# Attention with linear distance biases and a gated channel mix: softmax weights of tiles 9 to 23 transposed as rounded float32

## The chip, the core and the metric

The kernel is one program on one of the eight cores of a Trainium2 chip. The metric is device time in microseconds (us), from launch to end, as the median of several runs; lower is better. A profile of one further execution gives the times of single instructions. The engines are called PE (matrix products, with its weight loads shown apart as PEld), DVE (vectors), ACT (activation functions), POOL (general) and SP, which in this kernel issues almost all transfers. SPq, PEldq and so on are the instruction streams of these engines.

## What is computed

Four sequences of 768 positions pass through eight heads of causal attention of width 64, in which a query sees the last 96 keys and the first 8, with a bias that falls linearly with distance. The joined heads (512 wide) go through a channel mix.

```
scores = q @ k.T / 8 - slope[h] * dist       # outside the window: -1e9
a = exp(scores - max) / (sum + 1e-9)
x = (a @ v), heads joined                    # 4 x 768 x 512
xk = mu_k * x + (1 - mu_k) * x_prev          # xr likewise with mu_r
out = sigmoid(xr @ w_r) * (relu(xk @ w_k)**2 @ w_v)
```

## The kernel before

The 4 x 768 positions are 24 tiles of 128 queries (`NTILES`), six to a sequence. A tile needs two blocks of 128 keys: its own and the one before, in which the first 32 columns are replaced by the sequence's first keys. The first tile of a sequence (0, 6, 12, 18) needs one block only. Two tiles make a chunk, and the channel mix runs over 12 chunks of 256 positions.

A loop runs over steps; step n has four parts `hp` = 0 to 3, each for two heads. In a part PE does, in this order, the transposes of tile n-1 for the two heads (`transposes`, L331), the score products of tile n (`scores`, L298 to L302), and then a share of the channel mix of an earlier chunk (L391 to L393), taken from a generator piece by piece. At the start of a step PE multiplies the transposed weights of tile n-2 with the values (`weighted`, L348).

The path of one head's weights: PE writes the scores `s`; DVE adds the bias and takes the row's maximum (L309, into `e`); ACT takes the exponential and its sum (L310); DVE makes the reciprocal of the sums for four heads at a time (L316, L317); POOL multiplies the weights by it (L320). PE then transposes each 128 x 128 block of `e` into PSUM (`t`), ACT copies it out (`et`, L332), and PE multiplies. Up to tile 6 (`NATIVE` = 7) the scores are plain float32 products; from tile 7 on operands are split into a rounded part and a rest, both in the rounded float32 type (`F32R`), and a score takes two products (L301, L302). The channel mix takes three products of that type for each one.

In a transpose, `e` is the operand that is loaded into PE as weights, and the identity matrix `ident` streams past it; in the profile's rows the streamed operand is named first (`t<-ident,e`), and `s<-kw,qh` likewise has `qh` loaded and `kw` streamed.

Buffers of a pool go round. `e` has 10, one `kk` or `sig` of the channel mix takes one of 4 (`f2_pool`), and the split weights of the channel mix take 20 of the 21 of `w_pool` for the whole run once they are made, so that one is over.

SP issues its transfers strictly in the order of its list, and each waits there for what it needs: a load (`qraw`, `kraw`, `va`) for its buffer, an output (`out_dram<-sig`, L462) for the product before it. A scheduler places the instructions of every engine when the program is built; where it puts them is shown below in its own rows.

At the very end, seven small DVE instructions (L638 to L644) test the sizes of the window for a general path that these inputs don't need; each engine loads the result (L646) and branches over that path (L647).

Of the kernel before, what the change touches and what calls it, by code (L numbers as in the profile page):

```python
# [22 lines left out]
NTILES = B * NT  # L23
NCHUNK = NTILES // 2
NATIVE = 7
GMAX = 32
LMAX = 97
NEG = -1.0e9
# [4 lines left out]
def tile_biased_attention_channel_mix(ctx: ExitStack, tc: tile.TileContext, qT, kT, v, n_sizes, mu_kr, w_k, w_v, w_r, q_rows, k_rows, v_rows, slopes, out):  # L33
# [15 lines left out]
        vec.scalar_tensor_tensor(sizes, low, 0.0, high, op0=ALU.is_lt, op1=ALU.add)  # L49
        vec.scalar_tensor_tensor(sizes, sizes, 4294967296.0, low, op0=ALU.mult, op1=ALU.add)  # L50

    ident = const.tile([128, 128], F32, name="ident")
    make_identity(nc, ident)

    mus = const.tile([128, 2, 4], F32, name="mus")
    mus1 = const.tile([128, 2, 4], F32, name="mus1")
# [22 lines left out]
    ps_a = fast.enter_context(tc.tile_pool(name="ps_a", bufs=1, space=PSUM))  # L79
    ps_f = fast.enter_context(tc.tile_pool(name="ps_f", bufs=3, space=PSUM))  # L80


    zeros = const.tile([128, 256], BF16, name="zeros")
    vec.memset(zeros, 0.0)
# [89 lines left out]
    def weight_split(i):  # L174

        name, src, k, c = w_steps[i]
        word, hi = w_word.pop((name, k, c)), w_hi[name][:, k, c : c + 512]
        lo = w_low[name, k, c] = w_pool.tile([128, 512], F32R, tag="wl", name=f"w{name}_lo_{i}")
        (act.copy if i % 4 < 2 else pool_copy)(hi, word)
        if last[0] is None:  # L180
            vec.tensor_sub(lo, word, hi)  # L181
        else:
            with tc.issue_after(last[0]):
                vec.tensor_sub(lo, word, hi)

    w_count = [0, 0]
# [1 line left out]
    def weights_go(begun):  # L188
        while w_count[0] < min(begun, len(w_steps)):
            weight_begin(w_count[0])  # L190
            w_count[0] += 1
# [94 lines left out]
    def scores(n, hp):  # L286
# [31 lines left out]
        for u in range(nh):  # L318
            e = s["e"][h0 + u]
            pool.tensor_scalar(e[:, :w], e[:, :w], r[:, u : u + 1], 1.0, op0=ALU.mult, op1=ALU.mult)  # L320

    def transposes(n, hp):
        s = state[n]
        nb = 2 if n % NT else 1
        pt = ps_t.tile([128, 512], F32, name=f"t_{n}_{hp}", tag="t")
        et = et_pool.tile([128, 512], F32, name=f"et_{n}_{hp}", tag="et")
        for u in range(2):
            e = s["e"].pop(2 * hp + u)
            for k in range(nb):
                c = (u * nb + k) * 128  # L330
                pe.transpose(pt[:, c : c + 128], e[:, k * 128 : (k + 1) * 128], ident)  # L331
        act.copy(et[:, : 2 * nb * 128], pt[:, : 2 * nb * 128])  # L332
        s["et", hp] = et

# [45 lines left out]
            vec.scalar_tensor_tensor(x[:, j, :], xc[:, j, :], m[:, j : j + 1], x[:, j, :], op0=ALU.mult, op1=ALU.add)  # L380
        return x

    def channel_mix(xk, xr, out_rows, f_pool, f2_pool, ps_f, first=False):
        if first:
            kk_all = f_pool.tile([128, 8, 256], F32, name="kk_0", tag="kk_hi")
        else:
            kkh = f_pool.tile([128, 8, 256], F32R, name="kk_hi", tag="kk_hi")
            kkl = f_pool.tile([128, 8, 256], F32R, name="kk_lo", tag="kk_lo")

        def three(o, sh, sl, mh, ml, first, last):  # L390
            pe.matmul(o, sh, mh, start=first, stop=False)  # L391
            pe.matmul(o, sh, ml, start=False, stop=False)  # L392
            pe.matmul(o, sl, mh, start=False, stop=last)  # L393

        def z_of(i):
            z = ps_f.tile([128, 512], F32, name="z", tag="f")
            c = slice(i * 128, (i + 1) * 128)
            for k in range(4):
                if first:
                    pe.matmul(z, xr[:, k, c], w_word["r", k, 0], start=k == 0, stop=k == 3)  # L400
                else:
                    three(z, xr[0][:, k, c], xr[1][:, k, c], w_hi["r"][:, k, :], w_low["r", k, 0], k == 0, k == 3)
                yield
            sig = f2_pool.tile([128, 512], F32, name="sig", tag="f2")
            sigs.append((z, sig))

        sigs = []
        for fp in range(4):
            if first:
                weights_go(4 if fp < 2 else 8)  # L410
            else:
                splits_go(4 if fp < 2 else 8)
            ps = ps_f.tile([128, 512], F32, name="kp", tag="f")
            for u in range(2):
                f = slice((2 * fp + u) * 128, (2 * fp + u + 1) * 128)
                c = fp // 2 * 512
                g = slice(f.start - c, f.stop - c)
                o = ps[:, u * 256 : (u + 1) * 256]
                for k in range(4):
                    if first:  # L420
                        pe.matmul(o, w_word["k", k, c][:, g], xk[:, k, :], start=k == 0, stop=k == 3)
                    else:
                        three(o, w_hi["k"][:, k, f], w_low["k", k, c][:, g], xk[0][:, k, :], xk[1][:, k, :], k == 0, k == 3)
                    if k % 2:
                        yield
            kk = f2_pool.tile([128, 2, 256], F32, name="kk", tag="f2")
            pv = ps.rearrange("p (a q) -> p a q", a=2)
            act.activation(kk, pv, AF.Relu)  # L428
            if first:
                vec.tensor_mul(kk_all[:, 2 * fp : 2 * fp + 2, :], pv, kk)  # L430
                if fp % 2:
                    splits_ok[0] = 2 * fp + 2
            else:
                vec.tensor_mul(kk, pv, kk)  # L434
                act.copy(kkh[:, 2 * fp : 2 * fp + 2, :], kk)  # L435
                vec.tensor_sub(kkl[:, 2 * fp : 2 * fp + 2, :], kk, kkh[:, 2 * fp : 2 * fp + 2, :])  # L436
        if first:
            weights_go(12)
        else:
            splits_go(12)  # L440
        for i in range(2):
            yield from z_of(i)
        if first:
            splits_ok[0] = 12
        for z, sig in sigs:
            act.activation(sig, z, AF.Sigmoid)
        for i in range(2):
            c = slice(i * 128, (i + 1) * 128)
            vp = ps_f.tile([128, 512], F32, name="vps", tag="f")
            sig = sigs[i][1]  # L450
            for f in range(8):
                if first:
                    weights_go(13 + f)
                    pe.matmul(vp, kk_all[:, f, c], w_word["v", f, 0], start=f == 0, stop=f == 7)
                    if i:
                        splits_ok[0] = 13 + f
                else:
                    splits_go(13 + f)
                    three(vp, kkh[:, f, c], kkl[:, f, c], w_hi["v"][:, f, :], w_low["v", f, 0], f == 0, f == 7)
                yield  # L460
            last[0] = vec.tensor_mul(sig, vp, sig).ins
            nc.sync.dma_start(out_rows(i), sig)  # L462

    splits_ok = [0]
    last = [None]

    def ffn(c):
        xt = state["x", c]
        if c:
            xk, xr = (mix(xt[:, :, 1:257], xt[:, :, 0:256], tag, p4k, f_pool) for tag in "kr")  # L470
        else:
            xk, xr = (plain_mix(xt[:, :, 1:257], xt[:, :, 0:256], tag) for tag in "kr")
        return channel_mix(xk, xr, lambda i: out[(2 * c + i) * 128 : (2 * c + i + 1) * 128, :], f_pool, f2_pool, ps_f, c == 0)


    LAG = 3
# [17 lines left out]
    for step in range(NTILES + 1):  # L494
        if step + 1 < NTILES:
            load_tile(step + 1)
        if step < NTILES:
            load_v(step)
        for hp in range(4):
            if hp == 0 and step > 1:  # L500
                for i in range(4):
                    weighted(step - 2, i)
                global_v(step - 1)
            if step:
                transposes(step - 1, hp)
            if step < NTILES:
                scores(step, hp)
            if hp == 0:
                if step >= LAG and (step - LAG) % 2 == 0:
                    queue.append(ffn((step - LAG) // 2))  # L510
                    if len(queue) == 1 and step == LAG:
                        budget[0] = -17.5
            run_ffn(2.5)
            run_ffn(2.5)
            if hp == 1 and step + 1 < NTILES:
                split_tile(step + 1)
            slot = 4 * step + hp
            n = min(8, 2 + slot * 4 // 3) if slot < 6 else 8 + (slot - 5) * 6 // 7
            weights_go(n)
# [114 lines left out]

    okf = const.tile([128, 2], F32, name="okf")
    wide_i = const.tile([1, 1], I32, name="wide_i")
    with tc.issue_after(last[0]):
        vec.tensor_scalar(okf[:, 0:1], nlf, float(LMAX), None, op0=ALU.is_le)  # L638
        vec.tensor_scalar(okf[:, 1:2], nlf, 1.0, None, op0=ALU.is_ge)
        vec.tensor_mul(okf[:, 0:1], okf[:, 0:1], okf[:, 1:2])  # L640
        vec.tensor_scalar(okf[:, 1:2], ngf, float(GMAX), None, op0=ALU.is_le)
        vec.tensor_mul(okf[:, 0:1], okf[:, 0:1], okf[:, 1:2])
        vec.tensor_scalar(okf[:, 0:1], okf[:, 0:1], -1.0, 1.0, op0=ALU.mult, op1=ALU.add)
        vec.tensor_copy(wide_i, okf[0:1, 0:1])  # L644
# [48 lines left out]
```

## Time and profile before

| | |
|---|---|
| median of 3 runs (lowest to highest) | 518.22 us (517.7 to 520.34) |
| the profiled execution, its time / its span | 518.97 us / 517.2 us |
| PE, PEld busy | 498.5 us, 429.7 us |
| DVE, ACT, POOL busy | 359.2 us, 310.8 us, 252.8 us |
| transfers | 46.88 MB, mean 91 GB/s |

The span runs from the first to the last instruction; the rest of the execution's time lies around it. Busy time counts instructions, and matmuls overlap each other: the time that a matmul costs PE is the distance from its start to the next one's start, not its duration.

### The profile page before, as it was taken

What the parts mean: (1) busy time and instruction counts of PE and PEld (TensorE: products, weight loads), DVE (VectorE), ACT (ScalarE), POOL (GpSimd) and SP (SyncE); (2) the same over time, 40 slices, a digit from 0 to 9 for tenths busy, and PEclk for the clock granted to TensorE, in tenths of its full rate; (3) what the DMA queues carried; (4) which work ended last, traced back from release to release, by engine and by line L of the source; (5) the groups of instructions that cost most, each with busy time, mean ns of one, the idle gap of its engine ahead of it and who ended that gap; (6) DMA issues with size and microseconds to landing.
All of it is one profiled execution on the core that took longest, in us unless ns stands there. A gap on an engine that the chain in (4) does not pass through costs nothing.

```text
span 517.2 us, 9995 instructions
## 1 busy us (share of the span) xinstructions
PE 498.5 (96%) x3500; PEld 429.7 (83%) x3500; DVE 359.2 (69%) x862; ACT 310.8 (60%) x712; POOL 252.8 (49%) x392
## 2 busy tenths in 40 slices
PE   8797999999999999999999999999999999999993
PEld 6576765897898998998898998898898898898982
DVE  6889699977878668658678668658678666246321
ACT  5598365264588578467577578567577568453210
POOL 5668639259655635536646635526546615203000
PEclk9799999999999999999999999999999999999997
DMA  5996851403603603603603603603502300100001
GB/s 155 289 297 190 195 194 41 124 27 82 162 3 93 164 1 93 162 1 91 157 0 78 178 2 77 178 2 83 153 11 70 106 0 27 47 2 20 22 2 47
DMA packets 20538, 46.88 MB, mean 91 GB/s; under 512 B 3200, under 2 KB 5248, under 8 KB 20480
## 3 DMA queue, kind: packets, MB, share of 16 engines
q1 hardware_dynamic: 20336, 46.15, 32.4%
q8 instruction: 30, 0.49, 0.4%
q14 instruction: 28, 0.23, 0.1%
q10 hardware_dynamic: 144, 0.00, 0.0%
HBM read 39.85 MB, written 6.29 MB: 89 GB/s over the span
## 4 chain that ended last, share of the span: by engine, by line
PE 76%; DVE 9%; DMA 6%; POOL 3%; issue 2%; ACT 2%; SPq 0%; POOLq 0%; ACTq 0%; DVEq 0%
PE vps L392 7%; PE vps L391 7%; PE kp L391 7%; PE kp L392 7%; PE kp L393 7%; PE vps L393 7%; PE t L331 7%; PE av L348 7%; PE z L391 4%; PE z L392 4%; PE z L393 4%; PE s L302 3%; DMA ring<-in_kT_dram 3%; PE s L301 3%; DMA w<-in_w_v_dram 3%
## 5 line engine op out<-in xcount | busy, mean ns | idle before, releaser
L320 POOL TENSOR_SCALAR e<-e,r 128x256 f32<-128x256 f32 (+1 forms) x192 | 105.8, 568 | 144.6 <-DVE r L317 97.2
L310 ACT ACTIVATE e<-e,nmax 128x256 f32<-128x256 f32 (+1 forms) x192 | 92.9, 485 | 35.6 <-DVE nmax L309 34.0
L391 PE MATMUL kp<-xk_hi,wk_hi 128*128 128x256 f32 x352 | 99.5, 283 | 0.0
L393 PE MATMUL kp<-xk_hi,wk_lo 128*128 128x256 f32 x352 | 99.0, 281 | 0.0
L392 PE MATMUL kp<-xk_lo,wk_hi 128*128 128x256 f32 x352 | 98.7, 280 | 0.0
L309 DVE CUSTOM_DVE_ANT_0 e<-s,pat 128x256 f32<-128x256 f32 (+1 forms) x192 | 69.0, 396 | 31.4 <-PE s L302 22.3
L392 PE MATMUL vps<-wv_lo,kk_hi 128*128 128x512 f32 x176 | 70.0, 397 | 0.0
L391 PE MATMUL vps<-wv_hi,kk_hi 128*128 128x512 f32 x176 | 69.9, 397 | 0.0
L393 PE MATMUL vps<-wv_hi,kk_lo 128*128 128x512 f32 x176 | 69.2, 393 | 0.0
L391 PEld LDWEIGHTS kp<-xk_hi,wk_hi 128*128 128x128 f32 x352 | 66.3, 188 | 0.7 <-issue 0.2
L392 PEld LDWEIGHTS kp<-xk_lo,wk_hi 128*128 128x128 f32 x352 | 66.0, 188 | 0.7 <-DVE wr_lo L181 0.2
L393 PEld LDWEIGHTS kp<-xk_hi,wk_lo 128*128 128x128 f32 x352 | 66.1, 188 | 0.0
L434 DVE TENSOR_TENSOR kk<-kp,kk 128x512 f32<-128x512 f32 x44 | 30.4, 691 | 44.4 <-ACT kk L428 44.2
L332 ACT COPY et<-t 128x512 f32<-128x512 f32 (+1 forms) x96 | 52.3, 545 | 14.5 <-PE t L331 14.1
L331 PE MATMUL t<-ident,e 128*128 128x128 f32 x352 | 57.9, 281 | 2.7 <-POOL e L320 2.0
L331 PEld LDWEIGHTS t<-ident,e 128*128 128x128 f32 x352 | 41.8, 142 | 14.3 <-issue 4.1
L348 PE MATMUL av<-et,va 128*64 128x128 f32 x704 | 47.3, 280 | 1.9 <-ACT et L332 1.6
L348 PEld LDWEIGHTS av<-et,va 128*64 128x64 f32 x704 | 39.2, 137 | 9.4 <-issue 4.5
L436 DVE TENSOR_TENSOR kk_lo<-kk,kk_hi 128x512 fp32r<-128x512 f32 x44 | 32.8, 746 | 17.6 <-ACT kk_hi L435 17.6
L301 PE MATMUL s<-kw,qh 128*128 128x256 f32 (+1 forms) x136 | 40.6, 321 | 0.5 <-DVE kw L276 0.5
L428 ACT ACTIVATE kk<-kp 128x512 f32<-128x512 f32 x48 | 28.4, 591 | 20.1 <-PE kp L393 20.0
L393 PEld LDWEIGHTS vps<-wv_hi,kk_lo 128*128 128x128 f32 x176 | 33.1, 188 | 8.2
(113 smaller groups left out, 1036.3 us busy)
## 6 DMA issues: line engine op xcount, KB each, us to landing
kraw<-in_kT_dram SPq DMA_DIRECT2D x36, 256.0 KB, 4.1
qraw<-in_qT_dram SPq DMA_DIRECT2D x34, 256.0 KB, 4.3
va<-in_v_dram SPq DMA_DIRECT2D x24, 256.0 KB, 3.0
out_dram<-sig SPq DMA_DIRECT2D x24, 256.0 KB, 3.4
w<-in_w_k_dram SPq DMA_DIRECT2D x8, 512.0 KB, 7.8
w<-in_w_v_dram SPq DMA_DIRECT2D x8, 512.0 KB, 6.1
w<-in_w_r_dram SPq DMA_DIRECT2D x4, 512.0 KB, 9.1
qz<-in_qT_dram SPq DMA_DIRECT2D x14, 128.0 KB, 5.2
```

Of the source, the lines that this page charges most:

```text
L301: pe.matmul(o, s["qh"][:, h, :], s["kw"][:, h, c0:256], start=True, stop=False)
L309: vec.tensor_tensor_reduce(out=e[:, :w], in0=o, in1=p[:, h, :], op0=ALU.add, op1=ALU.min, scale=-0.125, scalar=3.0e38, accum_out=s["nmax"] ...
L310: act.activation(e[:, :w], e[:, :w], AF.Exp, bias=s["nmax"][:, h : h + 1], scale=-1.0, accum_out=s["sum"][:, h : h + 1])
L320: pool.tensor_scalar(e[:, :w], e[:, :w], r[:, u : u + 1], 1.0, op0=ALU.mult, op1=ALU.mult)
L331: pe.transpose(pt[:, c : c + 128], e[:, k * 128 : (k + 1) * 128], ident)
L332: act.copy(et[:, : 2 * nb * 128], pt[:, : 2 * nb * 128])
L348: pe.matmul(o, vt[:, h * 64 : (h + 1) * 64], et[:, c : c + 128], start=k == 0, stop=k == nb - 1)
L391: pe.matmul(o, sh, mh, start=first, stop=False)
L392: pe.matmul(o, sh, ml, start=False, stop=False)
L393: pe.matmul(o, sl, mh, start=False, stop=last)
L434: vec.tensor_mul(kk, pv, kk)
L436: vec.tensor_sub(kkl[:, 2 * fp : 2 * fp + 2, :], kk, kkh[:, 2 * fp : 2 * fp + 2, :])
```

## The change

Three edits.

First, from tile 9 on (`MOVED`) the weights of two heads are copied by two transfers from SP (`move`, L337) into one buffer of the rounded type, `e2`, bit by bit, and PE transposes out of that with an identity of the same type into the same PSUM tile viewed in that type. Parts 0 and 2 take the spare buffer of `w_pool`, parts 1 and 3 one of `f2_pool`. The identity is built in a buffer of `e` and copied by DVE. Second, the test for the general path is ordered after the fifth output product of the channel mix (`gates[4]`) and no longer after the last. Third, the last 128 rows of the last chunk are multiplied, gated and written in two halves of 256 columns.

```diff
+MOVED = 9
-    ident = const.tile([128, 128], F32, name="ident")
-    make_identity(nc, ident)
+    ident_r = const.tile([128, 128], F32R, name="ident_r")
+    ident = ident_r.bitcast(F32)
...
+    plain = e_pool.tile([128, 128], F32, name="plain", tag="e")
+    make_identity(nc, plain)
+    vec.tensor_copy(ident_r, plain)
...
+    def move(n, hp):
+        if n < MOVED:
+            return
+        s = state[n]
+        w = 256 if n % NT else 128
+        if hp % 2:
+            e2 = f2_pool.tile([128, 512], F32R, name=f"e2_{n}_{hp}", tag="f2")
+        else:
+            e2 = w_pool.tile([128, 512], F32R, name=f"e2_{n}_{hp}", tag="wl")
+        for u in range(2):
+            nc.sync.dma_start(e2[:, u * w : (u + 1) * w].bitcast(F32), s["e"][2 * hp + u][:, 0:w])
+        s["e2", hp] = e2
...
-                pe.transpose(pt[:, c : c + 128], e[:, k * 128 : (k + 1) * 128], ident)
+                if n < MOVED:
+                    pe.transpose(pt[:, c : c + 128], e[:, k * 128 : (k + 1) * 128], ident)
+                else:
+                    pe.transpose(pt[:, c : c + 128].bitcast(F32R), s["e2", hp][:, c : c + 128], ident_r)
...
+            w = 256 if last and i else 512
+            for o in range(0, 512, w):
+                d = slice(o, o + w)
...
-                    three(vp, kkh[:, f, c], kkl[:, f, c], w_hi["v"][:, f, :], w_low["v", f, 0], f == 0, f == 7)
+                        three(vp[:, d], kkh[:, f, c], kkl[:, f, c], w_hi["v"][:, f, d], w_low["v", f, 0][:, d], f == 0, f == 7)
...
-            last[0] = vec.tensor_mul(sig, vp, sig).ins
-            nc.sync.dma_start(out_rows(i), sig)
+                gates.append(vec.tensor_mul(sig[:, d], vp[:, d], sig[:, d]).ins)
+                nc.sync.dma_start(out_rows(i)[:, d], sig[:, d])
...
             if step:
+                if hp < 3:
+                    move(step - 1, hp + 1)
                 transposes(step - 1, hp)
             if step < NTILES:
                 scores(step, hp)
+                if hp == 3:
+                    move(step, 0)
...
-    with tc.issue_after(last[0]):
+    with tc.issue_after(gates[4]):
```

The order of PE's work stays: on PE, at the start of step 14, where tile 13 is transposed, the rows before are these (`av` is the product with the values, `t` the transposed weights, `s` the scores, `kp` the channel mix):

```order
L348 MATMUL av_12_3066<-et_12_3_3010,va_12_2592 64x128 x2
L331 MATMUL t_13_0_3078<-ident_62,e_13_0_2875 128x128 x2
L331 MATMUL t_13_0_3078<-ident_62,e_13_1_2878 128x128 x2
L301 MATMUL s_14_0_3085<-kw_14_2968,qh_14_2966 128x256
L302 MATMUL s_14_0_3085<-kw_14_2968,ql_14_2967 128x256
L301 MATMUL s_14_0_3085<-kw_14_2968,qh_14_2966 128x256
L302 MATMUL s_14_0_3085<-kw_14_2968,ql_14_2967 128x256
L391 MATMUL kp_3045<-xk_hi_2882,wk_hi_70 128x256
```

and the same place in the changed kernel:

```order
L369 MATMUL av_12_3119<-et_12_3_3060,va_12_2621 64x128 x2
L352 MATMUL t_13_0_3134<-ident_r_62,e2_13_0_3082 128x128 x4
L306 MATMUL s_14_0_3141<-kw_14_3015,qh_14_3013 128x256
L307 MATMUL s_14_0_3141<-kw_14_3015,ql_14_3014 128x256
L306 MATMUL s_14_0_3141<-kw_14_3015,qh_14_3013 128x256
L307 MATMUL s_14_0_3141<-kw_14_3015,ql_14_3014 128x256
L412 MATMUL kp_3098<-xk_hi_2926,wk_hi_66 128x256
```

Four transposes stand where four stood, out of one buffer instead of two, and nothing else of PE's order moved.

On SP, at the same time of the program, the loads of tile 16 and the outputs of a chunk stood like this before:

```order
L231 DMA qraw_16_3303<-in_qT_dram 64x1024
L462 DMA out_0_dram<-sig_2831 128x512
L231 DMA qraw_16_3303<-in_qT_dram 64x1024
L241 DMA kraw_16_3304<-in_kT_dram 64x1024 x2
L462 DMA out_0_dram<-sig_2913 128x512
```

In the changed kernel the new transfers of tile 13 stand between them:

```order
L236 DMA qraw_16_3368<-in_qT_dram 64x1024
L486 DMA out_0_dram<-sig_2872 128x512
L236 DMA qraw_16_3368<-in_qT_dram 64x1024
L337 DMA e2_13_0_3082<-e_13_0_2919 128x256
L337 DMA e2_13_0_3082<-e_13_1_2922 128x256
L337 DMA e2_13_1_3131<-e_13_2_2983 128x256
L337 DMA e2_13_1_3131<-e_13_3_2986 128x256
L246 DMA kraw_16_3369<-in_kT_dram 64x1024 x2
L486 DMA out_0_dram<-sig_2957 128x512
L337 DMA e2_13_2_3188<-e_13_4_3035 128x256
```

The loads of `kraw_16` and the output behind it now wait in SP's list behind four transfers that wait for POOL.

At the end of the program SP's list was this before, with the load of the test's result (`wide_i`) behind the last output:

```order
L462 DMA out_0_dram<-sig_5840 128x512
L462 DMA out_0_dram<-sig_5854 128x512
L646 TENSOR_LOAD wide_i_5926
L646 ISA x2
L647 COMPARE_AND_BRANCH
```

and is this now:

```order
L337 DMA e2_23_3_5707<-e_23_7_5555 128x256
L486 DMA out_0_dram<-sig_5772 128x512
L486 DMA out_0_dram<-sig_5830 128x512
L486 DMA out_0_dram<-sig_6022 128x512
L486 DMA out_0_dram<-sig_6036 128x256 x2
L675 COMPARE_AND_BRANCH
```

The load of the result went up SP's list by some 190 rows, to the moves of tile 9; the last output is two transfers of half the width, and the branch follows them directly.

## Rows read from the trace of the kernel before

**Rows 1.** The page: span, and busy time of each engine with its share.

```profile
span 517.2 us, 9995 instructions
PE 498.5 (96%) x3500; PEld 429.7 (83%) x3500; DVE 359.2 (69%) x862; ACT 310.8 (60%) x712; POOL 252.8 (49%) x392
```

**Rows 2.** Busy time of PE, PEld, DVE, ACT, POOL; clock, DMA share, GB/s.

```profile
250.00:350.00 100.00, 100.00 (x758) 90.24 (x757) 70.49 (x160) 65.62 (x150) 51.76 (x81) 1.00 0.30 77
```

**Rows 3.** The chain that ended last: start, length, what.

```profile
136.68 0.59 PE t L331 x4
...
258.30 0.44 PE t L331 x4
...
467.98 0.43 PE z L391
509.11 0.69 DVE sig L461
```

**Rows 4.** Groups by shape: busy us, mean ns of one.

```profile
L331 PE MATMUL t<-ident,e 128*128 128x128 f32 x352 | 57.9, 281 | 2.7 <-POOL e L320 2.0 <-ACT et L332 0.5
L331 PEld LDWEIGHTS t<-ident,e 128*128 128x128 f32 x352 | 41.8, 142 | 14.3 <-issue 4.1 <-POOL e L320 4.0 <-POOL w L167 0.6
```

**Rows 5.** Timeline around the transposes of tile 13, part 1: start, length, what.

```profile
257.78 0.28 PE L391 MATMUL kp<-xk_hi,wk_hi 128*128 128x256 f32 x1
257.90 0.28 PE L392 MATMUL kp<-xk_lo,wk_hi 128*128 128x256 f32 x1
...
258.01 0.29 PE L393 MATMUL kp<-xk_hi,wk_lo 128*128 128x256 f32 x1
258.03 0.47 PEld L331 LDWEIGHTS t<-ident,e 128*128 128x128 f32 x4
258.14 0.60 PE L331 MATMUL t<-ident,e 128*128 128x128 f32 x4
```

**Rows 6.** Timeline of PE where chunk 0 is multiplied as plain float32.

```profile
47.94 2.86 PE L421 MATMUL kp<-xk,word 128*128 128x256 f32 x12 [0.84 <-DVE xk L380]
```

**Rows 7.** Timelines of PEld: two loads into an idle PE, plain and for transposes.

```profile
41.61 0.30 PEld L298 LDWEIGHTS s<-ring,qz 128*128 128x128 f32 x2 [0.89 <-PE s L299]
...
46.65 0.20 PEld L331 LDWEIGHTS t<-ident,e 128*128 128x128 f32 x2 [1.11 <-POOL e L320]
```

**Rows 8.** Timeline of PEld: rounded score products of tile 12, 128 columns.

```profile
225.16 0.19 PEld L301 LDWEIGHTS s<-kw,qh 128*128 128x128 f32 x1
225.26 0.19 PEld L302 LDWEIGHTS s<-kw,ql 128*128 128x128 f32 x1
225.38 0.19 PEld L301 LDWEIGHTS s<-kw,qh 128*128 128x128 f32 x1
```

**Rows 9.** Timelines of POOL, SP and PE: weights ready, transfers issued, transposes of tile 13.

```profile
248.78 1.84 POOL L320 TENSOR_SCALAR e<-e,r 128x256 f32<-128x256 f32 x4 [6.44 <-DVE r L317]
...
247.66 0.47 SPq L231 DMA_DIRECT2D qraw<-in_qT_dram  x1
...
253.63 0.66 PE L331 MATMUL t<-ident,e 128*128 128x128 f32 x4
```

**Rows 10.** The same two of tile 15.

```profile
285.80 1.84 POOL L320 TENSOR_SCALAR e<-e,r 128x256 f32<-128x256 f32 x4 [4.86 <-ACT et L332]
...
293.29 0.66 PE L331 MATMUL t<-ident,e 128*128 128x128 f32 x4
```

**Rows 11.** Transfers issued from 235 to 275 us: KB each, median us to landing.

```profile
qraw<-in_qT_dram SPq DMA_DIRECT2D x5, 256.0 KB, 4.4
...
va<-in_v_dram SPq DMA_DIRECT2D x1, 64.0 KB, 2.4
```

**Rows 12.** The end: timeline, and the branches of L647 (duration ns; start us).

```profile
509.11 0.69 DVE L461 TENSOR_TENSOR sig<-vps,sig 128x512 f32<-128x512 f32 x1 [4.93 <-PE vps L393]
...
509.83 0.33 SPq L462 DMA_DIRECT2D out_dram<-sig  x1
...
510.72 0.14 DVE L644 CAST wide_i<-okf 1x1 int32<-1x1 f32 x1
...
L647 DVEq COMPARE_BRANCH  x1: 72/72/72, 511.5 to 511.5; - x1
L647 SPq COMPARE_BRANCH  x1: 45/45/45, 511.8 to 511.8; - x1
L647 DVEq EVENT_SEMAPHORE  x1: 21/21/21, 515.4 to 515.4; - x1
```

More of the change, by code (lines that the diff above doesn't have):

```diff
@@ L179, in weight_split @@
         (act.copy if i % 4 < 2 else pool_copy)(hi, word)
-        if last[0] is None:
+        if not gates:
             vec.tensor_sub(lo, word, hi)
         else:
-            with tc.issue_after(last[0]):
+            with tc.issue_after(gates[-1]):
                 vec.tensor_sub(lo, word, hi)
@@ L381, in plain_mix, with channel_mix @@
         return x
-    def channel_mix(xk, xr, out_rows, f_pool, f2_pool, ps_f, first=False):
+    def channel_mix(xk, xr, out_rows, f_pool, f2_pool, ps_f, first=False, last=False):
         if first:
@@ L450, in channel_mix @@
             sig = sigs[i][1]
[L451 to L458, printed above, removed]
-                    three(vp, kkh[:, f, c], kkl[:, f, c], w_hi["v"][:, f, :], w_low["v", f, 0], f == 0, f == 7)
-                yield
-            last[0] = vec.tensor_mul(sig, vp, sig).ins
-            nc.sync.dma_start(out_rows(i), sig)
+            w = 256 if last and i else 512
+            for o in range(0, 512, w):
+                d = slice(o, o + w)
+                for f in range(8):
+                    if first:
+                        weights_go(13 + f)
+                        pe.matmul(vp, kk_all[:, f, c], w_word["v", f, 0], start=f == 0, stop=f == 7)
+                        if i:
+                            splits_ok[0] = 13 + f
+                    else:
+                        splits_go(13 + f)
+                        three(vp[:, d], kkh[:, f, c], kkl[:, f, c], w_hi["v"][:, f, d], w_low["v", f, 0][:, d], f == 0, f == 7)
+                    yield
+                gates.append(vec.tensor_mul(sig[:, d], vp[:, d], sig[:, d]).ins)
+                nc.sync.dma_start(out_rows(i)[:, d], sig[:, d])
     splits_ok = [0]
-    last = [None]
+    gates = []
     def ffn(c):
@@ L472, in ffn @@
             xk, xr = (plain_mix(xt[:, :, 1:257], xt[:, :, 0:256], tag) for tag in "kr")
-        return channel_mix(xk, xr, lambda i: out[(2 * c + i) * 128 : (2 * c + i + 1) * 128, :], f_pool, f2_pool, ps_f, c == 0)
+        return channel_mix(xk, xr, lambda i: out[(2 * c + i) * 128 : (2 * c + i + 1) * 128, :], f_pool, f2_pool, ps_f, c == 0, c == NCHUNK - 1)
     LAG = 3
@@ L636, in tile_biased_attention_channel_mix @@
     wide_i = const.tile([1, 1], I32, name="wide_i")
-    with tc.issue_after(last[0]):
+    with tc.issue_after(gates[4]):
         vec.tensor_scalar(okf[:, 0:1], nlf, float(LMAX), None, op0=ALU.is_le)
```

## Prediction

> **What bounds the kernel now.** I read the page first. PE is busy for 96% of the span, the next engine, DVE, for 69% [rows 1]. A busy PE need not be the limit, since matmuls overlap, so the second look goes to a stretch in the middle: between 250 and 350 us PE has no idle time at all, while DVE, ACT and POOL are busy for 70, 66 and 52% and transfers for 30% [rows 2]. The third look is at the chain that ended last. From about 137 us to the last product it is PE alone, one instruction behind the other, and the only things besides are a DVE product at 509.11 and what comes after it [rows 3]. So from 137 us on a microsecond that PE saves is a microsecond of the kernel, and what is done beside PE costs nothing until PE waits for it. The transposes stand in that chain as pieces of 0.44 us for four [rows 3].
>
> **The transposes.** Tiles 9 to 23 are 15 tiles. Tiles 12 and 18 have one key block, so two transposes in a part; the other 13 have four. That makes 13 x 16 + 2 x 8 = 224 transposes in 52 groups of four and 8 of two.
>
> What does one cost? Four take 0.60 us of which the last one's own length is 0.28 [rows 5, 4], so starts are (0.60 - 0.28) / 3 = 0.107 apart; their four loads give (0.47 - 0.14) / 3 = 0.11 [rows 5, 4]. Two things could set this distance: 128 columns of the identity streaming past, or the load of 128 columns of weights.
>
> Streaming: in plain float32 twelve products of 256 columns take 2.86 us, at most 0.24 each [rows 6], so 0.12 or less for 128 columns: that fits the 0.11. In the rounded type 256 columns take 0.115 to 0.12, read from the starts 257.78, 257.90 and 258.01 [rows 5], half as much, so 128 columns take 0.06.
>
> Loading: when two loads meet an idle PE, the second starts as soon as the first is through. For plain scores the two rows of 0.30 us, less one load's 0.19 [rows 7, 8], show 0.11 a load; for transposes 0.20 less 0.14 [rows 7, 4] shows 0.06. A load for a transpose is thus twice as fast as an ordinary one of the same 128 columns, and today's transposes are bound by the streaming. The rounded type halves the streaming; what it makes of the load is the disputed point. The trace has no rounded load for a transpose. Its bounds are 0.06, if the transposing load stays as fast as it is, and 0.11, which rounded loads for ordinary products take: starts at 225.16, 225.26 and 225.38 [rows 8]. I take 0.06, since both plain and rounded ordinary loads cost 0.11, so the type made no difference to a load there and the transposing did.
>
> The Trainium skill speaks against this: its page "TensorE: Matmul & The Clock Gate", section "LDWEIGHTS (loading the stationary operand)", says that a load takes its number of columns divided by 1.2 GHz, whatever else. By that 128 columns take 107 ns in either type, and the sum of this part would be nothing. The trace agrees with it for the loads of scores and not for the pair of loads for transposes.
>
> Within a group of four, three distances shrink; the fourth is that to the score product behind, whose own load of 0.11 must follow [rows 8], so it stays. 52 x 3 + 8 x 1 = 164 distances x (0.11 - 0.06) = 8.2 us. If the fourth shrank too it would be 224 x 0.05 = 11.2; with loads at 0.11 it is 0.
>
> **The transfers that this needs.** Each part of each tile from 9 on gets two transfers, 120 of 128 KB in all less the halves of tiles 12 and 18, 14.7 MB over some 290 us or 50 GB/s. The engines of the transfers are 30% busy at 77 GB/s there [rows 2], so they have room. What matters is whether `e2` is there when PE comes. POOL finishes the four scalings of tile 13 at 248.78 + 1.84 = 250.62, the first two of them half way, at 249.70, and PE starts its transposes at 253.63: 3.9 us [rows 9]. Tile 15 has 286.72 to 293.29, 6.6 us [rows 10]. Read in the same way, tile 19 has 3.9 too, tiles 9 and 21 6.3 and 6.5, the others 7.3 to 11.7; parts 1 to 3 of a tile have 5.0 and more. A transfer's way from issue to landing lies between 2.4 us (64 KB) and 4.4 (256 KB, in a row of loads) in that stretch [rows 11]. The new ones are 128 KB; I take 3, which leaves 0.9 us at tiles 13 and 19 and more elsewhere: no wait. At 4.4 these two would wait 0.5 us each, 1 us in all. Tile 13's transfers also stand in the queue behind a `qraw` issued at 247.66 [rows 9], which should have landed by 252.1.
>
> What is late next: in SP's list `kraw` of tile 16 and the next output come behind moves that wait for POOL; these moves are out by 251, and the `kraw` waits for its buffer until later anyway. `e2` of parts 0 and 2 share one buffer, each freed two parts, some 9 us, before it is needed. In `f2_pool` a `kk` can get a buffer that held `e2`, but only of a group that PE has transposed one part earlier. I cost these at nothing; their cover is the slack just listed.
>
> **The end.** Before, DVE made seven small steps after the last gate, the last ending at 510.86; then the engines loaded the result and branched, SP at 511.8, DVE at 511.5 with its next instruction at 515.4, and the span ended at 517.2 [rows 12, 1]. The test now sits at the fifth gate, under a busy PE, where DVE has 30% free. SP's list goes from the last output straight to the branch. The last output leaves earlier by the half of a gate of 0.69 us, some 0.3, so its issue ends at 509.83 - 0.3 + 0.33 = 509.9 instead of 510.2 and SP branches at 509.9 instead of 511.8, 1.9 earlier. DVE's last gate ends at 509.5; if its load of the result, some 0.5 us, comes only then, it branches at 510.0 instead of 511.5, 1.5 earlier. I take 1.7, with 1.0 and 2.3 as bounds (one engine's branch being as slow as three at once, or faster). Halving the last product makes 48 matmuls of 256 columns out of 24 of 512; per column they cost the same within 3%, of 5.6 us, so at most 0.15, which I leave out. The extra DVE copy of the identity, about 0.3 us, runs while PE waits for its first loads.
>
> **The sum.** 8.2 + 1.7 = 9.9 us less. The profiled execution took 518.97, so 509.1 for one like it; the median of the runs shown is 0.75 lower, 518.22, which gives 508.3.
>
> **The rivals.**
>
> *The weight load binds.* The rounded transposes stand 0.11 apart, because the load takes 0.11 as in [rows 8] or because a transpose must move all 32 bits and streams no faster. PE gains nothing and only the end is left: 518.2 - 1.7 = 516.5. For it speaks that every rounded load in this trace takes 0.11; against it the 0.06 of [rows 7]. Chance 0.23. The Trainium skill's rule ("TensorE: Matmul & The Clock Gate", "LDWEIGHTS") would give this time.
>
> *Partial.* The rate is as I say, but some of tiles 9 to 23 wait 1 to 3 us in their first part, since transfers of 128 rows of 1 KB queue behind loads: 511 to 515, say 513. Chance 0.08.
>
> *The transfers are late, and it is slower.* If the way from the scaled weights to the landed copy takes 8 us (SP's list blocked by an entry that waits for PE, such as `va`), the first parts fall short by 4.1 at tiles 13 and 19, by 1.4 to 1.7 at 9, 15 and 21, by 0.7 at 11 and 17 and by 0.3 at 23: 14.5 us, and 508.3 + 14.5 = 522.8. It decides from about 7.3 us on, where the shortfalls reach the gain. Against it: landings of 2.4 to 4.4 [rows 11]. Chance 0.07.
>
> **How the numbers follow.** My forecast has the remaining 0.62. Its own range goes from 11.2 + 2.3 us less, 504.7, to 7.2 less (the wait of 1 us and an end of 1.0), 511. Less than 0.5%, 2.6 us, can hardly be told from no change here. Forecast and partial case are faster; so is a small part of the load-bound case, where the end gives more than 2.6. Faster 0.71, same 0.22, slower 0.07. To leave out no more than 2 in 10 the range must take in the load-bound case: 504.8 to 517.0. The prediction is 508.3.
>
> **What the changed profile would show.** Right: groups of four rounded transposes spanning 0.46 us or less, starts 0.06 apart; the chain of waits still PE alone; no idle time before `t` that a transfer ended; a step of the middle shorter by 0.6 us; about 6.4 us from the last gate's start to the end of the span, where it is 8.1 now. Wrong: starts still 0.11 apart (the load or the width of the data binds), idle PE before the transposes of tiles 13 and 19, or an engine that leaves its branch as late as before.

## The result, and the profile after

The changed kernel takes 512.79 us (median of 4 runs, 511.15 to 512.86) beside 518.29 us of the kernel before on the same chip: ratio 0.9884, 95% interval 0.9863 to 0.9904. That is 5.5 us or 1.1% between the medians, where 9.9 us were forecast. Timed once more later it gave 512.82 us, 0.9887 (0.9870 to 0.9905). The profiled execution took 512.86 us with a span of 510.9 us.

The page of the changed kernel, span and busy time, answers to [rows 1]; the window from 250 to 350 us to [rows 2].

```profile
span 510.9 us, 10385 instructions
PE 495.7 (97%) x3524; PEld 427.8 (84%) x3524; DVE 360.7 (71%) x864; ACT 309.7 (61%) x712; POOL 253.5 (50%) x392
```

```profile
250.00:350.00 100.00, 100.00 (x784) 89.99 (x784) 72.99 (x162) 65.65 (x147) 52.83 (x80) 1.00 0.46 130
```

PE still has no idle time in the middle, and transfers rose from 77 to 130 GB/s and from 30 to 46% without changing that. The chain that ended last (start, length, what), for [rows 3]:

```profile
174.19 1.95 PE av L369 x32
...
257.23 0.29 PE t L352 x4
...
462.39 1.95 PE av L369 x32
...
506.29 0.42 DVE sig L485
```

A group of four transposes in the chain shrank from 0.44 to 0.29 us. But that row ends with the last transpose, and the score product behind it has begun before, so the row overstates the gain. The timelines of PE and PEld around the transposes of tile 13, part 1 (start, length, what), show it beside [rows 5]:

```profile
257.07 0.45 PE L352 MATMUL t<-ident_r,e 128*128 128x128 f32 x4
257.36 0.35 PE L306 MATMUL s<-kw,qh 128*128 128x256 f32 x1
257.55 0.28 PE L307 MATMUL s<-kw,ql 128*128 128x256 f32 x1
```

```profile
256.97 0.41 PEld L352 LDWEIGHTS t<-ident_r,e 128*128 128x128 f32 x4
257.32 0.19 PEld L306 LDWEIGHTS s<-kw,qh 128*128 128x128 f32 x1
257.43 0.19 PEld L307 LDWEIGHTS s<-kw,ql 128*128 128x128 f32 x1
```

The same place in the kernel before goes on behind [rows 5] with these, a load and the second score product:

```profile
258.47 0.19 PEld L301 LDWEIGHTS s<-kw,qh 128*128 128x128 f32 x1
258.69 0.28 PE L302 MATMUL s<-kw,ql 128*128 128x256 f32 x1
```

The matmuls span 0.45 us, as forecast. But the loads, which run ahead of them, take 0.35 us from the first of the group to that of the score product behind it, where before it was 0.44 (258.47 - 258.03): 0.09 less, not 0.15. What counts for PE is the distance from the first transpose to the second score product: 257.55 - 257.07 = 0.48 us, where the trace of before has 258.69 - 258.14 = 0.55. A group of four saves 0.07 us, not 0.15. The groups by shape (busy us, mean ns of one, idle time before), for [rows 4], show that no transfer is waited for:

```profile
L352 PE MATMUL t<-ident_r,e 128*128 128x128 f32 x224 | 27.3, 242 | 0.0
L352 PEld LDWEIGHTS t<-ident_r,e 128*128 128x128 f32 x224 | 24.4, 140 | 6.7 <-issue 2.6
```

The rows' durations, 242 and 140 ns, are no price either: a load's 140 is nearly that of plain float32, 142 [rows 4], but the distance to the next one is not the same.

The end: a timeline, and the branches of L675 (duration in ns, start), for [rows 12].

```profile
502.68 0.43 DVE L485 TENSOR_TENSOR sig<-vps,sig 128x256 f32<-128x256 f32 x1 [2.13 <-PE vps L414]
...
503.16 0.38 PE L412 MATMUL vps<-wv_hi,kk_hi 128*128 128x256 f32 x1 [0.59 <-DVE sig L485]
```

```profile
L675 DVEq COMPARE_BRANCH  x1: 72/72/72, 506.9 to 506.9; - x1
L675 DVEq EVENT_SEMAPHORE  x1: 21/21/21, 509.9 to 509.9; - x1
L675 PEldq COMPARE_BRANCH  x1: 3358/3358/3358, 504.6 to 504.6; - x1
L675 SPq COMPARE_BRANCH  x1: 53/53/53, 507.1 to 507.1; - x1
L675 SPq EVENT_SEMAPHORE  x8: 17/17/17, 508.7 to 509.2; - x8
```

A gate is DVE's product of `vps` and `sig`. PE's branch of 3.4 us now begins under the last product and is over at 508.0. DVE's branch comes 0.6 us after the last gate's start and no longer 2.4, and DVE's next instruction 3.0 us later instead of 3.9. PE, though, waits 0.59 us for the gate of the first half.

Stretch by stretch, from the chains of both kernels, between the product `av` just ahead of tile 9's transposes and the `av` behind tile 23's. In the chain of the kernel before these two stand at:

```profile
174.38 1.95 PE av L348 x32
...
466.03 1.95 PE av L348 x32
```

| stretch | before | after | change | forecast |
|---|---|---|---|---|
| to the first of these `av` | 174.38 | 174.19 | -0.2 | 0 |
| from there to the last `av`: all rounded transposes | 291.65 | 288.20 | -3.45 | -8.2 |
| from the last `av` to the last gate | 43.08 | 43.90 | +0.8 | 0.15 at most, left out |
| last gate's start to the end of the span | 8.1 | 4.6 | -3.5 | -1.7 |
| span | 517.2 | 510.9 | -6.3 | -9.9 |

These are the spans of one execution each; the one before was 0.7 us slower than the median of its kernel, so they differ by more than the medians do.

The theory from here on: a rounded transpose in a row is bound by its load, which takes some 0.085 us, and not by its streaming of 0.06. The rivals: the rounded type gives all 8.2 us and the transfers take it back; or the rounded transpose has some other fixed price.

### The profile page after: what moved, and what is told of

The parts are those of the page before. It is cut to its first block, busy times and chain, and to the rows that moved or that the text cites. A ratio compares the mean times of both kernels' runs of the same rounds, so it can differ in the third digit from the quotient of the medians.

```text
span 510.9 us, 10385 instructions
## 1 busy us (share of the span) xinstructions
PE 495.7 (97%) x3524; PEld 427.8 (84%) x3524; DVE 360.7 (71%) x864; ACT 309.7 (61%) x712; POOL 253.5 (50%) x392
## 4 chain that ended last, share of the span: by engine, by line
PE 73%; DVE 11%; DMA 4%; issue 4%; POOL 4%; ACT 3%; SPq 0%; POOLq 0%; ACTq 0%; DVEq 0%
PE vps L412 7%; PE vps L413 7%; PE kp L414 7%; PE kp L412 7%; PE kp L413 7%; PE vps L414 7%; PE av L369 6%; PE z L412 4%; PE t L352 4%; PE z L413 4%; PE s L306 4%; PE z L414 4%; PE s L307 3%; DMA w<-in_w_v_dram 3%; DVE e L314 1%
## 5 line engine op out<-in xcount | busy, mean ns | idle before, releaser
L412 PE MATMUL vps<-wv_hi,kk_hi 128*128 128x512 f32 (+1 forms) x184 | 71.4, 388 | 0.6 <-DVE sig L485 0.6
L413 PE MATMUL vps<-wv_lo,kk_hi 128*128 128x512 f32 (+1 forms) x184 | 71.3, 387 | 0.0
L414 PE MATMUL vps<-wv_hi,kk_lo 128*128 128x512 f32 (+1 forms) x184 | 70.5, 383 | 0.0
L414 PEld LDWEIGHTS vps<-wv_hi,kk_lo 128*128 128x128 f32 x184 | 34.6, 188 | 7.9
L412 PEld LDWEIGHTS vps<-wv_hi,kk_hi 128*128 128x128 f32 x184 | 34.6, 188 | 7.5 <-DVE sig L485 0.8
L413 PEld LDWEIGHTS vps<-wv_lo,kk_hi 128*128 128x128 f32 x184 | 34.6, 188 | 6.0
```

## The experiments

### Transfers or transposes?

Two kernels keep the edits of the end. The first moves no tile; the second moves all tiles of the change, but transposes the copies in plain float32.

```diff
-MOVED = 9
+MOVED = 24
```

```diff
-                    pe.transpose(pt[:, c : c + 128].bitcast(F32R), s["e2", hp][:, c : c + 128], ident_r)
+                    pe.transpose(pt[:, c : c + 128], s["e2", hp][:, c : c + 128].bitcast(F32), ident)
```

Expected of the first: 

> No tile is moved (MOVED = 24), so all transposes stay plain and no copies are made; the two edits of the end stay. Theory: in the changed kernel the transposes gave 3.6 us between tile 9 and the last product with the values, the end gave 3.5, and the halved last product lost 0.8; so this one should be 2.7 us faster than before, about 515.6, and 2.8 to 3.6 slower than the changed kernel. Rival: the rounded transposes gave the whole 8.2 us of the prediction and their transfers took 4.6 of it back; this kernel would then look the same, and the kernel with copies and plain transposes tells the two apart.

Expected of the second: 

> All transfers and buffers of the changed kernel stay, but the transposes read the copies as plain float32. Theory: the transfers cost nothing, so this is the same as the kernel with the end's edits alone, about 515.6 (within 0.5), and its groups of four stand 0.109 apart again. Rival (the transfers cost 4.6 us by contention or late buffers): 520.2.

Measured: 515.94 us, ratio 0.9958 (0.9942 to 0.9975), and 515.69 us, 0.9954 (0.9937 to 0.9971). The chain that ended last of the first, and then of the second:

```profile
173.80 1.95 PE av L369 x32
465.46 1.95 PE av L369 x32
```

```profile
172.87 1.95 PE av L369 x32
...
256.79 0.44 PE t L352 x4
...
464.52 1.95 PE av L369 x32
```

The stretch of the transposes takes 291.66 and 291.65 us in these two and 291.65 before: 120 transfers that move 14.7 MB cost PE nothing in it, and the group of four is back at 0.44. The second kernel differs from the changed one in the type of the transposes alone, so the rounded type is worth 3.45 us, and the transfers take none of it back. The rival falls.

### The price of one transpose

Four kernels make something more in front of each of the 224 transposes of moved tiles, into the same place: the same transpose again, or one that loads only the first 64 columns (and so fills only 64 rows of the place) and streams the same 128 of the identity; each in the rounded type and in plain float32 (out of the copies).

```diff
+                    pe.transpose(pt[0:64, c : c + 128].bitcast(F32R), s["e2", hp][:, c : c + 64], ident_r)
                     pe.transpose(pt[:, c : c + 128].bitcast(F32R), s["e2", hp][:, c : c + 128], ident_r)
```

Rounded, whole: 

> Each of the 224 rounded transposes is made twice in a row into the same place. Theory: a rounded transpose in a row costs its load, 0.086 us, so 224 x 0.086 = 19.3 more than the changed kernel: 532.1. Rival, the prediction's distance of 0.06: 13.4 more, 526.2. Second rival, 0.109 as in plain float32: 24.4 more, 537.2.

Rounded, 64 columns loaded: 

> Before each of the 224 rounded transposes one that loads only the first 64 of its 128 columns, with the same 128 columns of the identity streamed. Theory (the load sets 0.086, the streaming only 0.06): the extra one costs about 0.06, 13.4 more than the changed kernel, 526.2. Rival (a rounded transpose takes 0.086 whatever it loads): as with the whole transpose, 532.1.

Plain, whole: 

> The copies are transposed in plain float32, and each transpose is made twice. Theory: 224 x 0.109 = 24.4 more than the kernel with copies and plain transposes (about 515.6): 540. Rival (a plain transpose costs its load of 0.057, seen when two meet an idle PE): 12.8 more, 528.4.

Plain, 64 columns loaded: 

> Plain float32; before each of the 224 transposes one that loads only 64 of its columns and streams all 128 of the identity. Theory (in plain float32 the streaming binds): no cheaper than a whole one, 24.4 more, 540. Rival (the load binds in plain float32 too): half of that or so, 528.

Measured, one run each; the stretch is that between the two `av` as above, and its excess is against the changed kernel (288.20) or the kernel with plain copies (291.65):

| added | time | first and last `av` | stretch | excess | each of 224 |
|---|---|---|---|---|---|
| rounded, whole | 531.32 | 172.99, 480.51 | 307.52 | 19.32 | 0.086 |
| rounded, 64 loaded | 526.21 | 174.14, 475.71 | 301.57 | 13.37 | 0.060 |
| plain, whole | 541.58 | 175.04, 491.11 | 316.07 | 24.42 | 0.109 |
| plain, 64 loaded | 540.55 | 174.28, 490.00 | 315.72 | 24.07 | 0.107 |

Halving the load makes a rounded transpose cheaper by 0.026 us and a plain one not. So the load sets the price of the rounded one, and not that of the plain one. That the streaming sets the plain one's is argued: 0.109 fits the 0.12 or less for 128 columns that the prediction reads from [rows 6], but no run changed the number of columns streamed. The timelines of PEld show the loads by themselves where they meet an idle PE, behind the `av` of tile 12; first rounded and whole, then rounded with 64 columns first:

```profile
256.26 0.14 PEld L352 LDWEIGHTS t<-ident_r,e 128*128 128x128 f32 x1 [0.17 <-issue]
256.34 0.14 PEld L353 LDWEIGHTS t<-ident_r,e 128*128 128x128 f32 x1
256.42 0.14 PEld L352 LDWEIGHTS t<-ident_r,e 128*128 128x128 f32 x1
```

```profile
255.92 0.11 PEld L352 LDWEIGHTS t<-ident_r,e 128*64 128x64 f32 x1 [0.17 <-issue]
255.97 0.14 PEld L353 LDWEIGHTS t<-ident_r,e 128*128 128x128 f32 x1
```

and the same place in plain float32, whole, and with 64 columns first:

```profile
260.43 0.14 PEld L352 LDWEIGHTS t<-ident_r,e 128*128 128x128 f32 x1 [0.17 <-issue]
260.49 0.14 PEld L353 LDWEIGHTS t<-ident_r,e 128*128 128x128 f32 x1
260.60 0.14 PEld L352 LDWEIGHTS t<-ident_r,e 128*128 128x128 f32 x1
```

```profile
259.52 0.11 PEld L352 LDWEIGHTS t<-ident_r,e 128*64 128x64 f32 x1 [0.17 <-issue]
259.55 0.14 PEld L353 LDWEIGHTS t<-ident_r,e 128*128 128x128 f32 x1
```

The second load follows the first by what the first takes: 0.08 rounded and 0.06 plain for 128 columns, 0.05 and 0.03 for 64. The first distance of the plain ones is the 0.06 of [rows 7]; from the third load on they stand 0.11 apart, so something other than the load before holds them. The rounded ones stay at 0.08 to 0.09 to the end of the group.

### The halved last product

PSUM is the memory that PE writes its products to. One kernel gives each half a PSUM tile of its own (`vps` is taken inside the loop over halves), one does not halve:

```diff
-            vp = ps_f.tile([128, 512], F32, name="vps", tag="f")
             sig = sigs[i][1]
             w = 256 if last and i else 512
             for o in range(0, 512, w):
                 d = slice(o, o + w)
+                vp = ps_f.tile([128, 512], F32, name="vps", tag="f")
```

```diff
-            w = 256 if last and i else 512
+            w = 512
```

Two tiles: 

> As the changed kernel, but each half of the last product has its own PSUM tile. Theory: the 0.87 us break of PE before the second half is the wait for the gate that still reads the shared tile; it goes, the second half starts 0.12 after the first, and the time falls by 0.8 to about 512.0. Rival (the break is the price of products of 256 columns, with twice as many loads): stays at 512.8.

Not halved: 

> As the changed kernel, but the last product is whole again. Theory: no break of 0.87 us, but a last gate of 0.69 us instead of 0.42: 0.6 less than the changed kernel, about 512.2, and 0.2 to 0.3 more than with two tiles. Rival (halving is a gain by itself): 0.3 more than the changed kernel, 513.1.

Measured: 510.94 us, ratio 0.9865 (0.9839 to 0.9890), and 511.70 us, 0.9881 (0.9855 to 0.9906). From the last `av` to the last gate the two take 43.05 and 43.09 us, as before the change (43.08), where the changed kernel takes 43.90. With two tiles the products of the second half follow without a break, and the last gate begins at 504.27; timeline of PE around the place where the halves meet, and the chain's last row:

```profile
501.12 0.28 PE L414 MATMUL vps<-wv_hi,kk_lo 128*128 128x256 f32 x1
501.24 0.28 PE L412 MATMUL vps<-wv_hi,kk_hi 128*128 128x256 f32 x1
```

```profile
461.22 1.95 PE av L369 x32
...
504.27 0.42 DVE sig L485
```

So products of 256 columns cost no more than half of one of 512, and the 0.8 us was the wait for the gate. Whether halving with two tiles gains anything over not halving can't be told from the times (510.94 and, below, 511.76 against 511.70). Since the medians of the changed kernel and of the one with two tiles differ by 1.9 us, more than that, these two were run again side by side:

Changed kernel: 

> The changed kernel itself once more, on the same chip and beside the same runs as the kernel with two PSUM tiles, since the two were timed apart. Theory: 512.8 as before; the rival, that the two do not differ, has both at one time.

Two tiles: 

> The kernel with a PSUM tile for each half again, beside the changed kernel. Theory: 0.86 us less than the changed kernel, all of it between the two halves of the last product, 511.9. Rival (the earlier difference of 1.9 was scatter of the start alone): the same time.

Measured: 512.82 us, 0.9887 (0.9870 to 0.9905), and 511.76 us, 0.9876 (0.9852 to 0.9899): 1.1 us apart, with intervals that overlap. The time alone does not prove the better kernel; the traces do for 0.85 us of it, in both pairs (43.90 and 43.90 against 43.05 and 43.05). The rest is the start: the first `av` of the stretch stands between 172.8 and 175.0 us in kernels that differ little up to there.

### The test at its old place

```diff
-    with tc.issue_after(gates[4]):
+    with tc.issue_after(gates[-1]):
```

> The changed kernel with the test for the general path ordered after the last output product again, as before. Theory: the whole of the end's gain but the half gate hangs on the test's place: from the start of the last gate to the end of the span 8.1 - 0.27 = 7.8 us instead of 4.6, so 3.2 us more than the changed kernel, 516.0. Rival, the prediction's term (1.7 for the end, 0.3 of it from the half gate): 1.4 more, 514.2.

Measured: 514.88 us, 0.9933 (0.9915 to 0.9952), about 2.1 us above the changed kernel and between the two expectations. From the start of the last gate (505.82) to the end of the span (512.9) are 7.1 us, against 4.6 with the early test: in this pair of traces the test's place is worth 2.5. In the other kernels with the early test that stretch takes 4.6 to 5.9 us, one trace each. Its branches:

```profile
L675 PEldq COMPARE_BRANCH  x1: 3878/3878/3878, 507.9 to 507.9; - x1
L675 DVEq COMPARE_BRANCH  x1: 72/72/72, 508.0 to 508.0; - x1
L675 DVEq EVENT_SEMAPHORE  x1: 21/21/21, 511.2 to 511.2; - x1
L675 PEldq EVENT_SEMAPHORE  x1: 51/51/51, 511.9 to 511.9; - x1
```

DVE branches 2.1 us after the last gate's start instead of 0.6, and is through it in 3.3 us instead of 3.0. But here PE comes out last: its branch takes 3.9 us, its next instruction stands at 511.9, and the span ends 1.0 us behind that, as it ends 1.0 us behind DVE's in the changed kernel. The kernel before needed 8.1. Of the 1.0 us between it and this kernel the half gate explains 0.27. The rest lies behind the branches: before, DVE came out last, 3.9 us after its branch [rows 12], and the end of the span followed 1.8 us later. Why was not settled.

### Two more tiles

With two PSUM tiles for the halves, tiles 7 and 8 are moved as well, through the buffers of `kk` and `sig` alone.

```diff
-MOVED = 9
+MOVED = 7
-        if hp % 2:
+        if hp % 2 or n < 9:
```

> Two PSUM tiles for the halves, and tiles 7 and 8 moved as well, all their copies in buffers of the channel mix's kk and sig. Theory: 8 more groups of four, 0.07 us each, 0.6 us less than the kernel with two tiles alone, 510.4. Rival (PE is not the only limit before tile 9, or the copies wait there for a buffer): the same as that kernel, 510.9, or more.

Measured: 512.93 us, 0.9894 (0.9875 to 0.9913): no gain, and 1 to 2 us above the two runs of the kernel with two tiles. The chain has a transfer in it, ahead of tile 7's first transposes:

```profile
134.60 3.10 DMA e<-e
...
137.84 0.56 PE t L352 x4
...
155.59 1.95 PE av L369 x32
...
175.14 1.95 PE av L369 x32
```

and PE's own timeline has the wait:

```profile
137.84 0.56 PE L352 MATMUL t<-ident_r,e 128*128 128x128 f32 x4 [0.74 <-DMA e<-e]
```

Tile 8 gains: 175.14 - 155.59 = 19.55 us, against 19.80 in the kernel with two tiles (153.22 to 173.02). Tile 7 has too little slack for the copy: read as in the prediction, its first weights were ready 2.0 us before PE took them in the kernel before, the copy takes 3.1, and PE waits 0.74 us. That wait alone is more than the 0.5 us that two tiles at 0.25 could give. How much of the rest is scatter of the start can't be told, and the end of this kernel is longer too (5.9 us from the last gate), for a reason that was not looked for.

## Why the prediction was right in sign and too large

**What bounds the kernel.** Right. From 137 us to the last product PE alone makes the chain in both kernels, but for the gate between the halves in the changed one, and 3.45 us saved in a stretch came out in full.

**The transposes, 8.2 us: measured 3.45.** The streaming did halve, but the term was mis-sized, and the step that failed is "I take 0.06, since both plain and rounded ordinary loads cost 0.11, so the type made no difference to a load there and the transposing did". The type does make a difference to a load for a transpose: 0.06 in plain float32, 0.085 in the rounded type. The streaming takes 0.06 or less, and the load, 0.085, took its place as the bound. The count of distances was nearly right: 164 x (0.109 - 0.086) = 3.8, and the stretch shows 3.45, 0.021 each. In the 15 groups behind an `av`, where the first load meets an idle PE, the distance from the first to the second load grew, from 0.058 to 0.085 (medians of the traces before and after), which takes off 0.4. The first distance of a group was no good sign: there the load had been made under the product ahead, and the transposes start 0.06 apart; the forecast's test "starts 0.06 apart" holds for two of the three distances of such a group and says nothing on the sum. The sign that told was the step of the middle: it became shorter by 0.26 us (19.80 to 19.54 from one `av` to the next), not by 0.6.

The Trainium skill's page "TensorE: Matmul & The Clock Gate", section "LDWEIGHTS (loading the stationary operand)", gives a formula by the number of columns alone, by which 107 ns for 128 columns is an estimate. The loads of scores agree, with 0.11 in both types; those for transposes do not, with 0.085 rounded and 0.058 plain. The Trainium skill's section "Back-to-back issue gap", on the same page, gives about 81 ns for each pair of a load and a matmul of 128 columns in a row. The trace agrees roughly, with 0.085 to 0.086 for the rounded ones, and does not for the plain ones, with 0.109.

**The transfers, nothing: measured nothing.** Their way is 3.0 us from 246 to 253 us, where tile 13's copies are made, as taken:

```profile
e<-e SPq DMA_DIRECT2D x4, 128.0 KB, 3.0
```

Of the rivals, "the weight load binds" had the right mechanism and the wrong price, and late transfers, whole or partial, happened in no tile from 9 on. They did at tile 7, which the change leaves alone. That 512.8 us is the time of the rival "Partial", 513, is a coincidence: no transpose of a moved tile waited for its copy.

**The halves, at most 0.15 and left out: measured +0.8.** The step looked at the price of a product only. It missed that both halves share a PSUM tile, so the second half's first product must wait until the gate of the first has read it.

**The end, 1.7 us: measured 3.5.** The branch of DVE came 1.8 us earlier relative to the last gate (1.5 had been worked out), and it took 0.9 us less. SP was through its own semaphores by 509.2, ahead of DVE's at 509.9, where before the last of them stood behind DVE's at 515.4 [rows 12]:

```profile
L647 SPq EVENT_SEMAPHORE  x8: 17/17/17, 512.3 to 515.8; - x8
```

That goes with the remaining 0.8. The bound of 2.3 was too low: it allowed for a somewhat faster branch, and not for work that had stood behind it to run beside it.

**The sum.** The transposes fell short by 4.75 us and the halves cost 0.8, while the end gave 1.8 more than forecast. So the total came nearer to the forecast than its main term did, and that is luck. The measured 512.8 us lies outside the forecast's own range and inside the full one only because that takes in the load-bound case. One step of the range is also added up wrongly: a wait of 1 us and an end of 1.0 leave 8.2 + 1.0 - 1.0 = 8.2 us, so 510.0, and not 7.2 and 511.

## What to carry to other kernels

Here a transpose in a row cost no less than its load, and halving the streaming helped only until the load bound; so price both in the new type before multiplying by the count. Judge a group of transposes by the distance to the second product behind it, not by the transposes' own rows. Where a product is split so that one half's reading lies beside the other half's making, give each half its own PSUM tile: here that turned 0.8 us lost into nothing lost, with 510.9 and 511.8 us for the kernel.

## What was unexpected

The load of a transpose depends on the type: 128 and 64 columns take 0.058 and 0.028 us in plain float32, 0.085 and 0.054 in the rounded type (medians of the distance from first to second load behind `av`, 15 groups each; the whole ones in the kernel with plain copies and in the changed kernel). That is 0.026 or 0.027 more for a load of either size. Why was not tried.

An engine's first instruction after the branch over the general path can come 3 us late. In the changed kernel DVE's comes 3.0 us after its branch, with no other work of DVE between, and PE's branch takes 3.4, though part of that lies under its last product. ACT's next one comes after 0.4. The Trainium skill's page "Runtime: NRT & Kernel Launch", section "Instruction fetch mechanics", says that a branch to code outside the window already fetched must wait for a fetch. The rows fit that, but no run here changed the distance of the jump.
